# Sliding-window attention in 64-key half-blocks: 76 score batches instead of 96

## The chip, the core and the metric

The kernel runs on one core of a Trainium2 chip. The core has a matrix engine (TensorE, PE in the profile, with PEld for its weight loads), a vector engine (VectorE, DVE), a scalar engine (ScalarE, ACT), GpSimd (POOL) and SyncE (SP), which here only issues transfers. Each engine takes its own instructions in order and waits for the others by semaphores. TensorE reads SBUF and writes PSUM, which has eight banks of 128 partitions x 512 fp32 values. GpSimd works on SBUF alone. The metric is the device time of one execution in microseconds; less is better.

## The reference

One layer on 2048 rows of 512 values: layer norm, then attention and a gated unit side by side, added to the input.

```python
H = 32; Dh = 16; W = 256
xn = _layernorm(x)                                  # (1, 2048, 512)
qkv = (xn @ wqkv).reshape(B, S, 3, H, Dh).transpose(2, 0, 3, 1, 4)
scores = einsum("bhqd,bhkd->bhqk", q, k) * Dh ** -0.5
mask = (i - j >= 0) & (i - j < W)                   # query i, key j
p = softmax(where(mask, scores, -1e9))
attn = einsum("bhqk,bhkd->bhqd", p, v).transpose(0, 2, 1, 3).reshape(B, S, D) @ wo
g, u = xn @ w_gate, xn @ w_up                       # F = 1792
out = x + attn + (g * u) @ w_down
```

All inputs and the output are bf16. A query sees its own key and the 255 before it, so a block of 128 keys is seen by three blocks of 128 queries: a lower triangle, a full block and an upper triangle.

## The kernel before

**Chunks and banks.** The 2048 rows are taken in four chunks T of 512, that is four blocks of 128. Q, K, V and the transposed normed input of a chunk stay in SBUF. PSUM is split by hand: four banks hold one batch of scores (`ps_s`, one buffer), one bank the value sums (`ps_a`, the tile `accb`), and three banks (`ps_m`) everything else, in turn.

**Score batches (`scores`, line 214).** Heads are taken eight at a time, as a group c of 128 channels, four at once: e = 0..3 sits in channels 32e to 32e + 31, and `par` says whether the first or the second 16 of these are used (Ko is K with the first 16 zeroed). A step is (T, c, par, i). For each of the three entries i of `GROUPS` it takes two (key block, first and last query block, column) parts, which together make up to 512 columns for each e. Four matmuls of a part, one for each e, work in four row tiles of the array and write four different banks. One exp over all columns (line 231) makes the strip P in SBUF, and GpSimd zeroes the triangles in P with `affine_select`, 128 columns x 4 at a time (lines 236 and 240). There are 24 steps a chunk, 96 in all; in the first chunk the parts with keys before row 0 are missing.

**Value phases (`values`, line 245).** After the third step of a (T, c, par), and two steps later (`LAG = 2`), its three strips are multiplied by V: six parts of 128 to 384 columns, four matmuls each, one in each column tile, summed in `accb`. V has a column of ones, so the sums of the softmax come out beside the values. VectorE then transposes `accb` (at, line 263), takes the reciprocal (rz, line 265), and `divide` (line 268) multiplies (on, line 276) and, for each second phase, transposes back into OT (line 279). There are 32 value phases.

**Fillers.** All other matmuls form a fixed list: the Q, K and V projections of a chunk, the gate and up products, the down product and the output projection. A gate bank is four matmuls of 512 columns and is copied to SBUF as gsb by VectorE (line 294); an up bank is multiplied with gsb into hT by VectorE (line 304); K and Q banks are copied by VectorE (lines 182 and 188, and Ko at line 183); V banks by ScalarE (line 169). Down and output projection share one bank for 18 matmuls (lines 317 and 323) and end in y, on VectorE (line 341). `run` (line 424) walks the steps and after each one calls `fill`, which takes items off the list until the work given out, in units of one filler matmul, reaches a due point: the total times the share of the steps' weights done so far. A score step counts `SCORES` = 1.85 and a value phase `VALUES` = 3.5. Some items carry a step before which they must be done, or a value phase after which they may start. So the order of every engine is fixed when the program is built; nothing is reordered on the chip except weight loads.

Of the kernel before, what the change touches and what calls it, by code (L numbers as in the profile page):

```python
# [12 lines left out]

GROUPS = (
    ((-2, 0, 0, 0), (0, 0, 2, 128)),
    ((-1, 0, 1, 0), (2, 2, 3, 256)),
    ((1, 1, 3, 0), (3, 3, 3, 384)),
)  # L20


class Kernel:
    def __init__(self, ctx, tc, x, wqkv, wo, wg, wu, wd, out):
        self.tc, self.nc = tc, tc.nc
        _, S, D = x.shape
        self.S, self.D, self.F = S, D, wg.shape[1]
        assert D == 512 and S % 512 == 0 and self.F % 256 == 0
        self.NT, self.NCH, self.NF = S // 128, S // 512, self.F // 128
        self.x_d, self.out_d = x.flatten_outer_dims(), out.flatten_outer_dims()  # L30
        self.w_d = dict(qkv=wqkv, o=wo, g=wg, u=wu, d=wd)

        def pool(name, bufs, **kw):
            return ctx.enter_context(tc.tile_pool(name=name, bufs=bufs, **kw))

        self.const = pool("const", 1)
        self.chunk2 = pool("chunk2", 2)
        self.chunk3 = pool("chunk3", 3)
        self.ppool = pool("ppool", 6)
        self.work = pool("work", 3)  # L40
        self.xpool = pool("xpool", 4)
        self.small = pool("small", 4)
        self.ypool = pool("ypool", 5)
        self.ps_s = pool("ps_s", 1, space=bass.MemoryType.PSUM)
        self.ps_a = pool("ps_a", 1, space=bass.MemoryType.PSUM)
        self.ps_m = pool("ps_m", 3, space=bass.MemoryType.PSUM)


    def setup(self):
# [44 lines left out]
        nc.vector.tensor_copy(out=self.odd[:], in_=podd[:])  # L94
        self.mhalf = const.tile([128, 4], F32, name="mhalf")
        nc.gpsimd.memset(self.mhalf[:], -0.5)
        self.xnT, self.Q, self.hT, self.O, self.OT = {}, {}, {}, {}, {}
        self.K, self.Ko, self.V = {}, {}, {}
        self.strips, self.at = {}, {}

    def new_chunk(self, T):

        self.Q[T] = self.chunk2.tile([128, 4, 512], BF16, tag="Q", name=f"Q{T}")
        self.K[T] = self.chunk3.tile([128, 4, 512], BF16, tag="K", name=f"K{T}")
        self.Ko[T] = self.chunk3.tile([128, 4, 512], BF16, tag="Ko", name=f"Ko{T}")
        self.V[T] = self.chunk3.tile([128, 4, 32, 18], BF16, tag="V", name=f"V{T}")
        self.nc.gpsimd.memset(self.V[T][:, :, :, 16:18], 1.0)


    def norm_stats(self, t, n=4):  # L110
# [79 lines left out]
    def first_chunk(self):  # L190

        self.new_chunk(0)
        for b in range(2):
            self.norm_stats(b, 1)
            self.norm_scale(b, 1)
        for b in range(4):
            self.norm_apply(b)
            if b < 2:
                self.norm_stats(b + 2, 1)
                self.norm_scale(b + 2, 1)  # L200
        self.norm_transpose(0, False)
        for b in range(4):
            if b < 3:
                self.norm_transpose(b + 1, False)
            self.proj_v(b)
        self.proj_qk(0, 0, 1)
        self.proj_qk(0, 0, 0, on_act=True)
        self.proj_qk(0, 1, 1)


    def parts(self, T, i):
        return [p for p in GROUPS[i] if 4 * T + p[0] >= 0]

    def scores(self, T, c, par, i):

        nc = self.nc
        parts = self.parts(T, i)
        S = self.ps_s.tile([128, 4, 512], F32, tag="S", name="S")
        for kb, q0, q1, col in parts:
            n, (U, j) = 128 * (q1 - q0 + 1), divmod(4 * T + kb, 4)  # L220
            for e in range(4):
                rows = slice(32 * e, 32 * e + (32 if par else 16))
                nc.tensor.matmul(S[:, e, col:col + n],  # L223
                                 lhsT=(self.Ko if par else self.K)[U][rows, c, 128 * j:128 * j + 128],
                                 rhs=self.Q[T][rows, c, 128 * q0:128 * q0 + n],
                                 start=True, stop=True, tile_position=(32 * e, 0),
                                 skip_group_check=True)
        P = self.ppool.tile([128, 4, 512], BF16, tag="P", name="P")
        lo = parts[0][3]
        hi = parts[-1][3] + 128 * (parts[-1][2] - parts[-1][1] + 1)  # L230
        nc.scalar.activation(out=P[:, :, lo:hi], in_=S[:, :, lo:hi], func=ACT.Exp, scale=0.25)  # L231
        for kb, q0, q1, col in parts:
            for q in range(q0, q1 + 1):
                j = col + 128 * (q - q0)
                if q == kb:
                    nc.gpsimd.affine_select(out=P[:, :, j:j + 128], in_=P[:, :, j:j + 128],  # L236
                                            pattern=[[0, 4], [1, 128]], compare_op=ALU.is_ge,
                                            fill=0.0, base=0, channel_multiplier=-1)
                elif q == kb + 2:
                    nc.gpsimd.affine_select(out=P[:, :, j:j + 128], in_=P[:, :, j:j + 128],  # L240
                                            pattern=[[0, 4], [-1, 128]], compare_op=ALU.is_gt,
                                            fill=0.0, base=0, channel_multiplier=1)
        self.strips[(T, c, par, i)] = P

    def values(self, T, c, par):


        nc = self.nc
        acc = self.accb
        first = True  # L250
        for i in range(3):
            P = self.strips.pop((T, c, par, i))
            for kb, q0, q1, col in self.parts(T, i):
                n, (U, v) = 128 * (q1 - q0 + 1), divmod(4 * T + kb, 4)
                for e in range(4):
                    nc.tensor.matmul(acc[32 * e:32 * e + 17, 128 * q0:128 * q0 + n],  # L256
                                     lhsT=self.V[U][:, v, 8 * c + 2 * e + par, 0:17],
                                     rhs=P[:, e, col:col + n], start=first, stop=(i == 2),
                                     tile_position=(0, 32 * e), skip_group_check=True)
                first = False  # L260

        at = self.work.tile([128, 16, 32], F32, tag="at", name="at")
        nc.vector.transpose(out=at.rearrange("p b r -> p (b r)"), in_=acc[:])  # L263
        rz = self.small.tile([128, 16], F32, tag="rz")
        nc.vector.reciprocal(out=rz[:], in_=at[:, :, 16])
        self.at[(T, c, par)] = at, rz
# [78 lines left out]
    def fillers(self):  # L345


        out = []
        NCH, NF, NG = self.NCH, self.NF, 24

        def add(cost, f, before=None, after=None):
            out.append((cost, f, before, after))
# [8 lines left out]
        def project(T):  # L361
            add(0, lambda: self.new_chunk(T))
            for b in range(4):
                for ks in halves:
                    add(2, lambda t=4 * T + b, ks=ks: self.proj_v(t, ks), NG * T)
            for c in range(4):
                qk(T, c, NG * T + 6 * c)

        def gu(T, between):
            for f in range(NF):  # L370
# [20 lines left out]
                add(2, lambda lo=lo: self.down(T, b, lo, lo + 2))  # L391

        def wo(T, b, cs):
            add(len(cs), lambda: self.wo(T, b, cs), None, NG * T + 6 * cs[-1] + 5)

        qk(0, 1, 6, (0,))
        for c in range(2, 4):
            qk(0, c, 6 * c)
        for T in range(NCH):
            todo = {}  # L400
            if T:
# [22 lines left out]
    def run(self):  # L424
        self.xns, self.stats, self.sums = {}, {}, {}
        self.setup()
        NCH, NG, LAG = self.NCH, 24, 2
        RESERVE = 38
        self.first_chunk()
        steps = [(T, c, par, i) for T in range(NCH) for c in range(4) for par in range(2) for i in range(3)]  # L430
        weight = [sum(p[2] - p[1] + 1 for p in self.parts(s[0], s[3])) + 1.7 for s in steps]
        SCORES, VALUES = 1.85, 3.5
        work = self.fillers()
        total = sum(w[0] for w in work) - RESERVE + SCORES * len(steps) + VALUES * (len(steps) // 3 - 1)
        done_w, spent, n = 0, 0, 0
        valued = -1

        def fill(upto, group):
# [11 lines left out]

        def values(g):
            nonlocal spent
            if g < 0 or steps[g][3] < 2:
                return False
            self.values(*steps[g][:3])
            spent += VALUES
            return True

        def divide(g):
            nonlocal valued  # L460
            self.divide(*steps[g][:3])
            valued = g

        for g, s in enumerate(steps):
            fill(-1, g)
            self.scores(*s)
            spent += SCORES
            done_w += weight[g]
            upto = total * done_w / sum(weight)
            if values(g - LAG):  # L470
                fill(min(spent + 4, upto), g)
                divide(g - LAG)
            fill(upto, g)
        T = NCH - 1
        fill(spent + 20, -1)
# [48 lines left out]
```

The softmax here doesn't subtract the row's maximum and nothing guards it: scores larger than these inputs give would overflow.

## Time and profile before

| | |
|---|---|
| median of 3 runs | 279.97 us (279.86 to 280.08) |
| span of the profiled execution | 277.8 us |
| time around the span, against the median | 2.2 us |
| score batches, value phases | 96, 32 |
| score and value matmuls | 704, 704 |
| TensorE instructions in the program | 4,830 |
| granted TensorE clock | full in all stages |

The profile is of one execution. Busy times of TensorE are modelled from the size of a matmul, and a matmul's own duration (0.38 us for 512 columns) is longer than the distance to the next one, since they overlap. Starts are what was recorded, so the cost of a run of matmuls is read here from the distances between starts. A group's row gives line, engine, operation, tiles and shape, the count, then busy time and the mean of one in ns, then the idle time of its engine ahead of it and what ended most of that.

The stages by time, from the lines that ran: Q, K and V of the first chunk to 19 us, then for each chunk gate and up (19 to 51, 88 to 119, 155 to 186 and 223 to 255 us), the next chunk's projections (to 67, 134 and 202 us) and the down products (to 88, 154 and 221 us); the last down products run to 273 us.

### The profile page before, as it was taken

The numbers are of one execution on the slowest core, as the hardware profiler recorded it, in microseconds if no ns is written. First come the engines' busy times: TensorE is split into PE (matmuls) and PEld (weight loads), VectorE is DVE, ScalarE is ACT, GpSimd is POOL, SyncE is SP. The second block draws the span as 40 slices with busy tenths as digits, with TensorE's granted clock in tenths as the row PEclk, the third lists the DMA queues.
The fourth block names the chain that finished last, engine by engine and source line by source line (L and its number), as shares of the span: only waits on it lengthen the run. The fifth ranks groups of instructions, "written<-read, shape, count | busy, mean of one in ns | idle before, by whom it ended". The sixth has DMA issues, their size and how long they took to land.

```text
span 277.8 us, 5829 instructions
## 1 busy us (share of the span) xinstructions
PE 269.4 (97%) x2396; PEld 115.0 (41%) x2414; DVE 188.1 (68%) x338; ACT 183.1 (66%) x121; POOL 164.3 (59%) x284
## 2 busy tenths in 40 slices
PE   7999999999999999999999999999999999999994
PEld 6433433433344434343444344444434444433453
DVE  6388989788567777858855778774853477777232
ACT  3666766786767666688666676769676766767601
POOL 4146666765786656574777656575656566656510
PEclk9999999999999999999999999999999999999999
DMA  6999511000111100000012200000001000000002
GB/s 211 377 371 348 113 21 21 19 2 0 39 40 57 21 2 0 1 2 0 2 40 61 53 2 2 0 2 1 0 2 40 19 21 1 2 0 2 0 2 76
DMA packets 17163, 13.74 MB, mean 49 GB/s; under 512 B 7025, under 2 KB 17137, under 8 KB 17137
## 3 DMA queue, kind: packets, MB, share of 16 engines
q1 hardware_dynamic: 16848, 13.18, 15.6%
q8 instruction: 19, 0.31, 0.5%
q10 hardware_dynamic: 288, 0.20, 0.2%
q14 instruction: 8, 0.06, 0.1%
HBM read 9.70 MB, written 2.10 MB: 42 GB/s over the span
## 4 chain that ended last, share of the span: by engine, by line
PE 89%; ACT 5%; DVE 3%; issue 1%; DMA 1%; POOL 0%; ACTq 0%
PE up L300 18%; PE gp L289 18%; PE psd L317 18%; PE S L223 11%; PE qkp L177 9%; PE accb L256 8%; PE psd L323 5%; ACT P L231 3%; PE vp L165 3%; ACT V L169 1%; DMA x<-in_A_x_dram 1%; DVE st L116 1%; DVE hT L304 0%; DVE gsb L294 0%; PE xTp L151 0%
## 5 line engine op out<-in xcount | busy, mean ns | idle before, releaser
L231 ACT ACTIVATE P<-S 128x2048 bf16<-128x2048 f32 (+2 forms) x96 | 170.0, 1771 | 74.3 <-PE S L223 62.6
L236 POOL TENSOR_SCALAR_AFFINE_SELECT P<-P 128x512 bf16<-128x512 bf16 x128 | 84.7, 662 | 54.3 <-ACT P L231 54.1
L240 POOL TENSOR_SCALAR_AFFINE_SELECT P<-P 128x512 bf16<-128x512 bf16 x112 | 72.5, 647 | 38.4 <-ACT P L231 38.4
L300 PE MATMUL up<-xnT,Wu 128*128 128x512 bf16 x224 | 60.0, 380 | 0.1
L289 PE MATMUL gp<-xnT,Wg 128*128 128x512 bf16 x224 | 59.7, 380 | 0.0
L317 PE MATMUL psd<-Wd,hT 128*128 128x512 bf16 (+1 forms) x225 | 52.3, 366 | 1.4 <-issue 1.1
L263 DVE STREAM_TRANSPOSE at<-accb 128x512 f32<-128x512 f32 x32 | 22.8, 713 | 39.0 <-PE accb L256 39.0
L304 DVE TENSOR_TENSOR hT<-up,gsb 128x512 bf16<-128x512 f32 x56 | 38.1, 680 | 7.8 <-PE up L300 5.8
L294 DVE CAST gsb<-gp 128x512 bf16<-128x512 f32 x56 | 37.9, 676 | 5.9 <-PE gp L289 5.8
L317 PEld LDWEIGHTS <-hT 128*128 128x128 bf16 x238 | 21.5, 98 | 24.9 <-issue 4.7
L289 PEld LDWEIGHTS <-Wg 128*128 128x128 bf16 x224 | 20.0, 98 | 26.1 <-issue 5.2
L177 PE MATMUL qkp<-xnT,Wqkv 128*128 128x512 bf16 x128 | 30.6, 380 | 0.0
L300 PEld LDWEIGHTS <-Wu 128*128 128x128 bf16 x224 | 19.6, 98 | 26.4 <-issue 7.0
L256 PE MATMUL accb<-P,V 128*17 128x384 bf16 (+2 forms) x704 | 25.3, 276 | 0.0
L341 DVE TENSOR_TENSOR y<-psd,x 128x512 bf16<-128x512 f32 (+1 forms) x15 | 9.9, 666 | 17.9 <-PE psd L323 16.5
L223 PE MATMUL S<-Q,K 16*128 16x256 bf16 (+2 forms) x352 | 18.4, 276 | 0.5
L223 PE MATMUL S<-Q,Ko 32*128 32x256 bf16 (+2 forms) x352 | 18.4, 275 | 0.5 <-ACT P L231 0.2
L276 DVE TENSOR_TENSOR on<-at,rz 128x256 bf16<-128x256 f32 x32 | 18.1, 565 | 0.4
L177 PEld LDWEIGHTS <-Wqkv 128*128 128x128 bf16 x128 | 11.4, 98 | 14.6 <-issue 2.7
L256 PEld LDWEIGHTS <-V 128*17 128x17 bf16 x704 | 13.8, 90 | 8.7 <-issue 5.3
L182 DVE CAST K<-qkp 128x512 bf16<-128x512 f32 x16 | 11.0, 688 | 8.9 <-PE qkp L177 8.6
L323 PE MATMUL psd<-Wo,OT 128*128 128x512 bf16 (+1 forms) x67 | 16.6, 367 | 0.2 <-issue 0.2
(39 smaller groups left out, 141.1 us busy)
## 6 DMA issues: line engine op xcount, KB each, us to landing
Wg<-in_B_w_gate_dram SPq DMA_DIRECT2D x2, 896.0 KB, 10.1
Wu<-in_B_w_up_dram SPq DMA_DIRECT2D x2, 896.0 KB, 11.6
Wd<-in_B_w_down_dram SPq DMA_DIRECT2D x1, 1792.0 KB, 15.9
out_dram<-y SPq DMA_DIRECT2D x14, 128.0 KB, 1.7
Wqkv<-in_A_wqkv_dram SPq DMA_DIRECT2D x3, 512.0 KB, 5.5
x<-in_A_x_dram SPq DMA_DIRECT2D x1, 1024.0 KB, 10.5
x<-in_A_x_dram SPq DMA_DIRECT2D x1, 512.0 KB, 10.9
Wo<-in_A_wo_dram SPq DMA_DIRECT2D x1, 512.0 KB, 15.9
```

The source lines that it names most:

```text
L177: nc.tensor.matmul(ps[:], lhsT=self.Wqkv[:, k, lo:lo + 128], rhs=self.xnT[T][:, :, k, :], start=(k == 0), stop=(k == 3))
L223: nc.tensor.matmul(S[:, e, col:col + n], lhsT=(self.Ko if par else self.K)[U][rows, c, 128 * j:128 * j + 128], rhs=self.Q[T][rows, c, 128 ...
L231: nc.scalar.activation(out=P[:, :, lo:hi], in_=S[:, :, lo:hi], func=ACT.Exp, scale=0.25)
L236: nc.gpsimd.affine_select(out=P[:, :, j:j + 128], in_=P[:, :, j:j + 128], pattern=[[0, 4], [1, 128]], compare_op=ALU.is_ge, fill=0.0, base ...
L240: nc.gpsimd.affine_select(out=P[:, :, j:j + 128], in_=P[:, :, j:j + 128], pattern=[[0, 4], [-1, 128]], compare_op=ALU.is_gt, fill=0.0, bas ...
L256: nc.tensor.matmul(acc[32 * e:32 * e + 17, 128 * q0:128 * q0 + n], lhsT=self.V[U][:, v, 8 * c + 2 * e + par, 0:17], rhs=P[:, e, col:col + ...
L289: nc.tensor.matmul(ps[:], lhsT=self.Wg[:, k, 128 * f:128 * f + 128], rhs=self.xnT[T][:, :, k, :], start=(k == 0), stop=(k == 3))
L294: nc.vector.tensor_copy(out=self.gsb[:], in_=ps[:])
L300: nc.tensor.matmul(ps[:], lhsT=self.Wu[:, k, 128 * f:128 * f + 128], rhs=self.xnT[T][:, :, k, :], start=(k == 0), stop=(k == 3))
L304: nc.vector.tensor_tensor(out=self.hT[T][:, f, :], in0=ps[:], in1=self.gsb[:], op=ALU.mult)
L317: nc.tensor.matmul(ps, lhsT=self.hT[T][:, f, 128 * b:128 * b + 128], rhs=self.Wd[:, f, c0:c1], start=(f == 0), stop=False)
L323: self.nc.tensor.matmul(ps, lhsT=self.OT[T][:, c, 128 * b:128 * b + 128], rhs=self.Wo[:, c, c0:c1], start=False, stop=(c == 3))
```

## The change

Scores are taken over half-blocks of 64 keys. Half h of a key block uses the 64 array columns from 64h on, so a matmul works in a tile of 32 rows x 64 columns, eight of which exist (four e, two halves). A half-block is seen by 320 queries in place of 384 for a whole block: a triangle of 64, 256 full, a triangle of 64. Both halves are placed so that the same column of the strip is the same query in the full part.

There are now three kinds of batches, each 4 x 512 columns. EVEN and ODD belong to one `par` and hold key blocks J - 2, J and J + 2 for J = 0 or 1 (the rest of older blocks included); PLAIN holds, for both `par` at once, two full 128 x 128 blocks. A chunk has EVEN, ODD (par 0), PLAIN, EVEN, ODD (par 1) for each c, the first chunk only the four others: 4 x 4 + 3 x 4 x 5 = 76 steps.

The masks change. VectorE takes the minimum of two 64-column triangles with a constant table `diag` of zeros and 2^126 in one instruction; GpSimd's `affine_select` does the others, 64 columns x 4 each, four in a batch (three in the first chunk). PLAIN batches are not masked.

Where a strip column belongs to different queries in the two halves, the value product needs only one of them. For this there are zero-padded copies of V: Vu holds the first 64 keys of each block and zeros for the rest, Vl0 and Vl1 (even and odd chunks) the last 64. `zero_halves` fills the zeros once on GpSimd, and `copy_halves` copies the half of each chunk's V on VectorE. A value phase has 16 pieces of 64 to 256 columns in place of six (12 in the first chunk, in place of four).

The planner counts every step alike: the due point after step g is the total times (g + 1) / 76. The pools work and ypool each have one buffer less.

```diff
-GROUPS = (
-    ((-2, 0, 0, 0), (0, 0, 2, 128)),
-    ((-1, 0, 1, 0), (2, 2, 3, 256)),
-    ((1, 1, 3, 0), (3, 3, 3, 384)),
-)
+EVEN, ODD, PLAIN = 0, 1, 2
+BIG = 2.0 ** 126
...
-        self.work = pool("work", 3)
+        self.work = pool("work", 2)
...
-        self.ypool = pool("ypool", 5)
+        self.ypool = pool("ypool", 4)
...
+    def zero_halves(self, j):
+
+        for h in (0, 1) if j == 0 else (1,):
+            self.nc.gpsimd.memset(self.Vh[j][h][64 - 64 * h:128 - 64 * h], 0.0)
+
+    def copy_halves(self, T):
+
+        for h in range(2):
+            rows = slice(64 * h, 64 * h + 64)
+            self.nc.vector.tensor_copy(out=self.Vh[T % 2][h][rows], in_=self.V[T][rows])
...
+    def batches(self, T):
+
+        if T == 0:
+            return [(EVEN, 0), (ODD, 0), (EVEN, 1), (ODD, 1)]
+        return [(EVEN, 0), (ODD, 0), (PLAIN, None), (EVEN, 1), (ODD, 1)]
+
+    def score_pieces(self, T, kind, par):
+
+        if kind == PLAIN:
+            return [(p, kb, h, q, 128, 256 * p + col)
+                    for p in range(2) for kb, q, col in ((-1, 0, 0), (2, 384, 128)) for h in (None,)]
+        J, q = kind, 128 * kind
+        if T == 0:
+            first = [(par, 2, 0, 384 + 64 * J, 64, 0), (par, 2, 1, 384 + 64 * J, 64, 0)]
+            second = [(par, J, 1, q + 64, 64, 64)]
+        else:
+            first = [(par, J - 2, 0, q, 64, 0), (par, J - 2, 1, q, 128, 0)]
+            second = []
+        return first + second + [
+            (par, J, 0, q, 320, 64), (par, J, 1, q + 64, 320, 128),
+            (par, J + 2, 0, q + 256, 128, 384), (par, J + 2, 1, q + 320, 64, 448)]
...
+        for p, kb, h, q, n, col in self.score_pieces(T, kind, par):
+            U, j = divmod(4 * T + kb, 4)
+            keys, outs = slice(128 * j, 128 * j + 128), slice(0, 128)
+            if h is not None:
+                keys, outs = slice(128 * j + 64 * h, 128 * j + 64 * h + 64), slice(64 * h, 64 * h + 64)
             for e in range(4):
-                rows = slice(32 * e, 32 * e + (32 if par else 16))
-                nc.tensor.matmul(S[:, e, col:col + n],
-                                 lhsT=(self.Ko if par else self.K)[U][rows, c, 128 * j:128 * j + 128],
-                                 rhs=self.Q[T][rows, c, 128 * q0:128 * q0 + n],
-                                 start=True, stop=True, tile_position=(32 * e, 0),
+                rows = slice(32 * e, 32 * e + (32 if p else 16))
+                nc.tensor.matmul(S[outs, e, col:col + n],
+                                 lhsT=(self.Ko if p else self.K)[U][rows, c, keys],
+                                 rhs=self.Q[T][rows, c, q:q + n],
+                                 start=True, stop=True, tile_position=(32 * e, outs.start),
                                  skip_group_check=True)
...
+        both = P.rearrange("p e (b x) -> p e b x", x=64)[:, :, 1:7:5, :]
+        m = self.diag[:, 0:2, :] if T == 0 else self.diag[:, 1:3, :]
+        nc.vector.tensor_tensor(out=both, in0=both, in1=m.unsqueeze(1).to_broadcast([128, 4, 2, 64]),
+                                op=ALU.min)
+        for col in (320,) if T == 0 else (0, 320):
+            nc.gpsimd.affine_select(out=P[:, :, col:col + 64], in_=P[:, :, col:col + 64],
...
+        for col in (128, 448):
+            nc.gpsimd.affine_select(out=P[:, :, col:col + 64], in_=P[:, :, col:col + 64],
...
+    def value_pieces(self, T, kind, par):
+
+        if kind == PLAIN:
+            return [(256 * par, 2, -1, 0, 128), (256 * par + 128, 2, 2, 384, 128)]
+        J, q = kind, 128 * kind
+        if T == 0:
+            first = [(0, 2, 2, 384 + 64 * J, 64)]
+        else:
+            first = [(0, 2, J - 2, q, 64), (64, 1, J - 2, q + 64, 64)]
+        return first + [(64, 0, J, q, 64), (128, 2, J, q + 64, 256), (384, 1, J, q + 320, 64),
+                        (384, 0, J + 2, q + 256, 64), (448, 2, J + 2, q + 320, 64)]
...
+            V = self.V[U] if h == 2 else self.Vh[U % 2][h]
+            for e in range(4):
+                nc.tensor.matmul(acc[32 * e:32 * e + 17, q:q + n],
+                                 lhsT=V[:, v, 8 * c + 2 * e + par, 0:17],
+                                 rhs=P[:, e, col:col + n], start=(i == 0), stop=(i == len(todo) - 1),
+                                 tile_position=(0, 32 * e), skip_group_check=True)
...
-            done_w += weight[g]
-            upto = total * done_w / sum(weight)
+            upto = total * (g + 1) / len(steps)
             if values(g - LAG):
                 fill(min(spent + 4, upto), g)
                 divide(g - LAG)
+                T, c, par = due[g - LAG]
+                if (c, par) == (3, 1):
+                    self.copy_halves(T + 1)
             fill(upto, g)
```

## The prediction

> **What bounds the kernel now.** I read the busy times first, then the chain that ended last, then the costliest groups, one stretch of TensorE in order of time, and the stages.
>
> ```profile
> PE 269.4 (97%) x2396; PEld 115.0 (41%) x2414; DVE 188.1 (68%) x338; ACT 183.1 (66%) x121; POOL 164.3 (59%) x284
> PE 89%; ACT 5%; DVE 3%; issue 1%; DMA 1%; POOL 0%; ACTq 0%
> ```
>
> TensorE is busy almost all the time and is 89% of the chain; no transfer is on it. So only what shortens or interrupts TensorE moves the end, and time taken from ScalarE (66%) or GpSimd (59%) alone is worth nothing.
>
> ```profile
> L231 ACT ACTIVATE P<-S 128x2048 bf16<-128x2048 f32 (+2 forms) x96 | 170.0, 1771 | 74.3 <-PE S L223 62.6
> L236 POOL TENSOR_SCALAR_AFFINE_SELECT P<-P 128x512 bf16<-128x512 bf16 x128 | 84.7, 662 | 54.3 <-ACT P L231 54.1
> L300 PE MATMUL up<-xnT,Wu 128*128 128x512 bf16 x224 | 60.0, 380 | 0.1
> L304 DVE TENSOR_TENSOR hT<-up,gsb 128x512 bf16<-128x512 f32 x56 | 38.1, 680 | 7.8 <-PE up L300 5.8
> L294 DVE CAST gsb<-gp 128x512 bf16<-128x512 f32 x56 | 37.9, 676 | 5.9 <-PE gp L289 5.8
> ```
>
> The last column matters: TensorE waits 0.1 us before all 224 up matmuls, so VectorE always empties the banks in time today. VectorE never waits for an exp; only GpSimd (the masks) does.
>
> ```profile
> 100.83 0.59 PE L289 MATMUL gp<-xnT,Wg 128*128 128x512 bf16 x2
> 101.36 0.40 PE L223 MATMUL S<-Q,K 16*128 16x256 bf16 x8
> 101.68 0.83 PE L256 MATMUL accb<-P,V 128*17 128x128 bf16 x24
> 102.45 0.61 PE L289 MATMUL gp<-xnT,Wg 128*128 128x512 bf16 x2
> ```
>
> A score batch takes 0.32 us from its first start to the next phase's, a value phase 0.77. Over all 96 batches and 32 value phases the starts add to 30.5 and 24.8 us. Filler matmuls of 512 columns start 0.216 us apart. Four matmuls on the four row or column tiles start within some 10 ns and stream together, so 512 columns of a batch are 0.213 us of streaming; the other 0.11 is the change of array shape, and the filler run after it pays about 0.11 more.
>
> ```profile
> 19.00:51.00 32.00, 31.85 (x267) 12.44 (x266) 28.89 (x54) 20.62 (x16) 21.52 (x38) 1.00 0.45 130
> 88.00:119.00 31.00, 30.96 (x295) 12.73 (x292) 23.53 (x39) 21.33 (x12) 18.70 (x31) 1.00 0.04 10
> ```
>
> These are the first two gate/up stages (length, then busy PE, PEld, DVE, ACT, POOL). VectorE is at 90% in the first and 76% in the second, against 68% over the span.
>
> **The change, part by part.** The sum starts at 280.0, the median of the runs; the profiled span is 277.8, so 2.2 lie around it, and I leave those alone.
>
> *Batches, 76 for 96.* Twenty batches fewer save two shape changes each, 20 x 0.22 = 4.5 us. Streamed columns per row tile fall from 72 x 512 + 8 x (384 + 256 + 512) = 46,080 to 76 x 512 = 38,912 if the two halves stream at once: 7,168 / 2.4 per ns = 3.0 us. Together -7.5. If the halves stream one after the other, 64 batches take 0.213 longer: +13.6. The trace has no tile of 64 columns; the nearest rows, four row tiles or four column tiles, overlap fully, so I take overlap and keep the other end.
>
> *More and shorter matmuls.* Score matmuls go from 704 to 1,792 (24 or 28 in a half-block batch, 16 in a plain one), value matmuls from 704 to 1,920 (16 pieces a phase, 12 in the first chunk, for 6 and 4), each with a weight load. Their columns stay 1,536 per full value phase, so what is added is per piece. A set of four 128-column value matmuls takes 61 ns for 53 of streaming, longer ones 3 ns over. There are 24 x 10 + 8 x 8 = 304 more sets: 0.8 us at 2.5 ns; 10.3 us if a 64-column set (27 ns) can be no shorter than the 61 of the shortest seen. I take 5 ns, 1.5 us, as streaming set every interval seen, and 1 us for starting 24 score matmuls in place of 8.
>
> The Trainium skill's page "TensorEngine Tiling (Array Packing)", section Instruction Overhead, speaks against this part: about 60 cycles for each matmul whatever its size, so small free sizes gain nothing. By it, as an estimate, 3,712 small matmuls cost 93 us, some 40 over what I count. The rows above pay it once a set, not once a matmul, and I go by them.
>
> TensorE alone: 280.0 - 7.5 + 2.5 = 275.0.
>
> *ScalarE and GpSimd.* Exps: 76 x 1.88 = 143 us for 170. Masks: 240 selects of 256 elements for 240 of 512; at 0.29 us for 128 elements and 0.65 for 512, about 0.41, so 98 us for 157. Both are off the chain and worth nothing. The zero fills and the mask table add some 5 us on GpSimd at the start (0.33 us for 256 elements, two fills of 2,304 there), before the first values need them; at most 1 us shows.
>
> *VectorE: a new instruction that waits.* Each of 64 half-block batches gets a `min` of 512 bf16 elements with a table. Rows: 0.44 us (Ko, one tensor in) to 0.68 (hT, two, one from PSUM); I take 0.55, the other 512-element SBUF row (xn). 64 x 0.55 = 35 us. The copies into zero-padded V are 8 of 2,304 elements: 1.5 us each at Ko's slope, 3.0 at a PSUM cast's; 12 us, at chunk borders, where down matmuls need little of VectorE. VectorE goes from 188 to 235 us. The Trainium skill's page "VectorE: DVE Perf Modes" (perf-mode tier table) lets bf16 tensor_tensor in SBUF run at 2x; by it I estimate 0.42 for the `min`, 8 us less in all.
>
> The `min` stands in VectorE's queue right after its batch, so it waits for that batch's exp: in the trace exp starts about 0.53 after the first score matmul and takes 1.88, so the `min` cannot start for 2.4 us. Behind it are queued at, rz, and the gsb, hT, K and Q copies of everything that TensorE makes meanwhile. TensorE has three banks for that, 0.86 us each, and then stands. That is the cover, and I count whether it holds stage by stage, in the built order:
>
> - First gate/up stage: 10 `min`, 27 copies at 0.68, 5 value tails (at 0.71, rz 0.25, on 0.57), 2 OT, four norms: 38.5 us of VectorE. TensorE: 112 x 0.216 + 10 x 0.43 + 5 x 0.87 = 32.9. Over by 5.6.
> - The other three: 28.0, 29.5, 30.9 against TensorE's 30.7, 31.6, 32.0: 91 to 97% with in-order waits. A cycle worked by hand: scores end at 0, `min` 2.1 to 2.65, three copies to 4.7; TensorE has filled three banks by 2.6, does the next batch and wants the first bank at 3.0, free at 3.4: 0.4 lost. With a value tail ahead of the copies it is about 1.5, partly won back a batch later. Some 2 us per five batches, 10 batches a stage: 4 each, of which I take 3.5 for catching up, 10.5 in all.
> - Q/K projections: eight banks are 6.9 us of TensorE and 4 x (0.69 + 0.44 + 0.68) = 7.2 of VectorE before any `min`: 1 us in each of three chunks, 3 in all.
>
> Sum +19, with ends 3 (a `min` of 0.44, banks absorb nearly all) and 31 (0.68, no catching up). 275 + 19 = **294 us**.
>
> *Bookkeeping.* Due points are per step now, SCORES and VALUES unchanged; two work buffers for three and four y buffers for five cost nothing while gsb is used up within two banks. No DMA is added, and SP's queue keeps its order.
>
> **The rivals.**
> - *Faster: the banks absorb it.* If `min` costs 0.44 and VectorE's backlog hides the wait for exp, TensorE's sum stands: 275. For it: 0.1 us waited before 224 up matmuls today, and ScalarE freer. Against: 38.5 in 32.9 us cannot be absorbed.
> - *Slower by TensorE's instruction supply.* TensorE's instructions go from 4,830 to 9,438, and a batch with its value phase from 64 to 176. The densest stretch seen is those 64 in 1.09 us, 17 ns each, at streaming's pace. It decides from 1.09 / 176 = 6.2 ns an instruction on. At 12 ns: 2.1 for 1.09 us in 32 clusters (+33) and 0.58 for 0.33 in 44 lone batches (+11); with some VectorE stall left (6), 325. At 17 ns it would be 357. For it: no sustained rate beyond 58 ns is in the trace. Against: no wait of that kind shows in the dense stretches.
> - *Halves not at once.* +13.6, less 4 of VectorE's stall that then hides: 304.
>
> **How the numbers follow.** Forecast 0.47 (own range 283 to 306), absorbed 0.20, no change 0.03, supply 0.17, halves 0.13. The time is the forecast's, 294. The range 276 to 325 leaves out the better half of the absorbed case and the worse half of supply, some 0.2. Runs of this kernel differ by 0.1%, so 0.2% is what can be told from no change. Faster 0.20, same 0.03, slower 0.77.
>
> **What would show it.** Right: the gate/up and Q/K groups of TensorE get idle time released by gsb, hT, K or Q, several us in all; the `min` row shows idle before it released by ScalarE; VectorE passes 85%; TensorE's share of the span falls. A score batch of about 0.33 us and a value phase near 0.8 confirm streaming; 0.55 for the batch means halves in turn; 1.5 or more for the value phase means supply. Wrong: idle before gate and up matmuls stays near 0.1 us and the time is below 279.

## The result and the profile after

The changed kernel takes 317.5 us (median of four runs, 316.7 to 319.2); the kernel before took 280.0 beside it. The ratio is 1.135, with a 95% interval of 1.132 to 1.139: slower by 37.5 us. The profiled execution has a span of 317.1 us.

First the lines of its page that answer to those shown of before: busy times, the chain, then the groups.

```profile
PE 279.7 (88%) x4718; PEld 130.0 (41%) x4718; DVE 210.0 (66%) x410; ACT 156.6 (49%) x101; POOL 130.9 (41%) x291
...
PE 48%; DVE 26%; ACT 21%; issue 2%; POOL 2%; DMA 1%; ACTq 0%
...
L269 ACT ACTIVATE P<-S 128x2048 bf16<-128x2048 f32 x76 | 142.6, 1877 | 136.5 <-PE S L263 100.1
...
L278 DVE TENSOR_TENSOR P<-P,diag 128x512 bf16<-128x512 bf16 x64 | 27.9, 436 | 83.4 <-ACT P L269 83.4
L358 PE MATMUL up<-xnT,Wu 128*128 128x512 bf16 x224 | 59.7, 381 | 10.0 <-DVE gsb L352 9.7
L347 PE MATMUL gp<-xnT,Wg 128*128 128x512 bf16 x224 | 60.5, 384 | 6.7 <-DVE hT L362 6.6
...
L195 PE MATMUL qkp<-xnT,Wqkv 128*128 128x512 bf16 x128 | 32.7, 392 | 6.9 <-DVE Q L206 4.7
...
L381 PE MATMUL psd<-Wo,OT 128*128 128x512 bf16 (+1 forms) x68 | 17.6, 371 | 3.8 <-DVE OT L337 3.8
```

TensorE is no longer the bound: 88% busy and only 48% of the chain, where it was 89%. No other engine is full either. VectorE is at 66%, less than before's 68%. The row of L278 points to the reason: the new `min` is only 27.9 us of work, but VectorE stood idle 83.4 us ahead of it, all of it for exp. The last column of TensorE's rows shows who paid. The gate, up, Q and K matmuls now wait for the VectorE copies that free their banks (hT, gsb, Q), and the output projection waits for OT. The up matmuls waited 0.1 us before and 10.0 now.

One such wait in the changed kernel's timeline (start, length, engine, operation; the bracket is the idle time ahead and its releaser):

```profile
86.26 1.88 ACT L269 ACTIVATE P<-S 128x2048 bf16<-128x2048 f32 x1 [2.00 <-PE S L263]
...
87.11 0.81 PE L381 MATMUL psd<-Wo,OT 128*128 128x512 bf16 x3
88.17 0.43 DVE L278 TENSOR_TENSOR P<-P,diag 128x512 bf16<-128x512 bf16 x1 [2.03 <-ACT P L269]
...
88.51 0.71 DVE L321 STREAM_TRANSPOSE at<-accb 128x512 f32<-128x512 f32 x1
...
89.25 0.25 DVE L323 RECIPROCAL rz<-at 128x16 f32<-128x16 f32 x1
89.54 0.42 DVE L334 TENSOR_TENSOR on<-at,rz 128x256 bf16<-128x256 f32 x1
90.00 0.71 DVE L337 STREAM_TRANSPOSE OT<-on 128x512 bf16<-128x512 bf16 x1
...
90.77 0.61 PE L381 MATMUL psd<-Wo,OT 128*128 128x512 bf16 x1 [2.84 <-DVE OT L337]
```

The value phase had ended at about 86.7, so `at` could have begun then. But the `min` stood ahead of it until exp ended at 88.14. All four instructions of the tail came after it, and TensorE waited 2.84 us for OT.

Windows of the changed kernel (length, then busy time and count of PE, PEld, DVE, ACT, POOL; granted TensorE clock as a share of full speed, DMA share, GB/s); the first two are wide stretches, the last three were picked out by their clock:

```profile
16.00:56.00 40.00, 33.90 (x580) 14.98 (x583) 31.34 (x61) 18.43 (x10) 16.40 (x35) 0.96 0.43 132
72.00:92.00 20.00, 14.22 (x214) 5.87 (x212) 15.42 (x29) 7.01 (x4) 9.34 (x18) 0.87 0.01 2
...
21.80:25.20 3.40, 3.40 (x9) 1.05 (x7) 2.84 (x6) 0.00 (x0) 0.06 (x1) 0.51 1.10 347
76.40:79.90 3.50, 3.50 (x82) 1.56 (x79) 2.45 (x5) 0.74 (x1) 0.00 (x0) 0.51 0.02 5
90.10:96.90 6.80, 6.13 (x29) 2.13 (x30) 3.80 (x7) 1.88 (x1) 0.93 (x3) 0.50 0.15 39
```

In three stretches, 13.7 us together, the clock granted to TensorE was half. Each begins within 1.3 us of the end of a long wait of TensorE, so these waits were paid twice. With TensorE busy for most of those stretches, this is up to 6 or 7 us of this execution, the slowest of the four (319.2 us, mean clock 0.976). The fastest, 316.7 us, has 0.986: 3.2 us less of missing clock (the span times what the clock lacks of 1) go with 2.5 us less time. In the executions of run 6 below, 1.8 us of missing clock cost 1.6 to 1.8 us. The two middle executions lack 5.0 and 6.0 us of clock; by these two rates the clock is an estimated 4 to 5.5 us of the median's 37.5.

What the change did to the matmuls themselves is seen in one score batch and value phase of the changed kernel:

```profile
107.42 0.43 PE L263 MATMUL S<-Q,K 16*64 16x64 bf16 x24
107.77 0.32 PE L315 MATMUL accb<-P,V 128*17 128x128 bf16 x12
107.92 0.20 PE L315 MATMUL accb<-P,Vl 128*17 128x64 bf16 x4
107.95 0.20 PE L315 MATMUL accb<-P,Vu 128*17 128x64 bf16 x4
...
108.56 0.82 PE L381 MATMUL psd<-Wo,OT 128*128 128x512 bf16 x3
```

From start to next start, 24 score matmuls take 0.35 us and the 64 value matmuls 0.79. A set of four 64-column matmuls starts about 0.03 us after the one before.

### The profile page after: what moved, and what is told of

It is laid out like the page before. It is cut to its first block, busy times and chain, and to the rows that moved or that the text cites. A ratio compares the mean times of both kernels' runs of the same rounds, so it can differ in the third digit from the quotient of the medians.

```text
span 317.1 us, 10496 instructions
## 1 busy us (share of the span) xinstructions
PE 279.7 (88%) x4718; PEld 130.0 (41%) x4718; DVE 210.0 (66%) x410; ACT 156.6 (49%) x101; POOL 130.9 (41%) x291
## 4 chain that ended last, share of the span: by engine, by line
PE 48%; DVE 26%; ACT 21%; issue 2%; POOL 2%; DMA 1%; ACTq 0%
ACT P L269 21%; PE psd L375 16%; PE S L263 7%; PE up L358 6%; PE gp L347 6%; DVE at L321 4%; DVE P L278 4%; PE psd L381 4%; PE qkp L195 4%; DVE gsb L352 3%; PE accb L315 3%; DVE hT L362 3%; DVE OT L337 2%; PE vp L183 2%; DVE on L334 2%
## 5 line engine op out<-in xcount | busy, mean ns | idle before, releaser
L269 ACT ACTIVATE P<-S 128x2048 bf16<-128x2048 f32 x76 | 142.6, 1877 | 136.5 <-PE S L263 100.1
L281 POOL TENSOR_SCALAR_AFFINE_SELECT P<-P 128x256 bf16<-128x256 bf16 x112 | 57.3, 530 | 149.4 <-ACT P L269 149.4
L278 DVE TENSOR_TENSOR P<-P,diag 128x512 bf16<-128x512 bf16 x64 | 27.9, 436 | 83.4 <-ACT P L269 83.4
L375 PE MATMUL psd<-Wd,hT 128*128 128x512 bf16 (+1 forms) x238 | 56.3, 380 | 1.2 <-DVE hT L362 0.6
L285 POOL TENSOR_SCALAR_AFFINE_SELECT P<-P 128x256 bf16<-128x256 bf16 x128 | 54.5, 447 | 0.0
L352 DVE CAST gsb<-gp 128x512 bf16<-128x512 f32 x56 | 37.5, 670 | 0.7 <-PE gp L347 0.7
L358 PEld LDWEIGHTS <-Wu 128*128 128x128 bf16 x224 | 20.6, 98 | 37.5 <-issue 15.8
L315 PE MATMUL accb<-P,V 128*17 128x64 bf16 (+2 forms) x960 | 26.5, 222 | 0.0
L315 PE MATMUL accb<-P,Vu 128*17 128x64 bf16 x512 | 21.0, 194 | 0.0
L315 PEld LDWEIGHTS <-V 128*17 128x17 bf16 x960 | 17.3, 92 | 5.1 <-issue 0.7
L315 PE MATMUL accb<-P,Vl 128*17 128x64 bf16 x448 | 19.1, 194 | 0.0
L263 PE MATMUL S<-Q,Ko 32*64 32x64 bf16 (+3 forms) x896 | 17.5, 239 | 0.0
L263 PE MATMUL S<-Q,K 16*64 16x64 bf16 (+3 forms) x896 | 17.3, 237 | 0.0
## 6 DMA issues: line engine op xcount, KB each, us to landing
Wd<-in_B_w_down_dram SPq DMA_DIRECT2D x1, 1792.0 KB, 15.8
Wo<-in_A_wo_dram SPq DMA_DIRECT2D x1, 512.0 KB, 15.8
```

Of the source, the lines that this page charges most:

```text
L263: nc.tensor.matmul(S[outs, e, col:col + n], lhsT=(self.Ko if p else self.K)[U][rows, c, keys], rhs=self.Q[T][rows, c, q:q + n], start=True ...
L269: nc.scalar.activation(out=P[:], in_=S[:], func=ACT.Exp, scale=0.25)
L278: nc.vector.tensor_tensor(out=both, in0=both, in1=m.unsqueeze(1).to_broadcast([128, 4, 2, 64]), op=ALU.min)
L281: nc.gpsimd.affine_select(out=P[:, :, col:col + 64], in_=P[:, :, col:col + 64], pattern=[[0, 4], [-1, 64]], compare_op=ALU.is_gt, fill=0.0 ...
L285: nc.gpsimd.affine_select(out=P[:, :, col:col + 64], in_=P[:, :, col:col + 64], pattern=[[0, 4], [1, 64]], compare_op=ALU.is_ge, fill=0.0, ...
L315: nc.tensor.matmul(acc[32 * e:32 * e + 17, q:q + n], lhsT=V[:, v, 8 * c + 2 * e + par, 0:17], rhs=P[:, e, col:col + n], start=(i == 0), st ...
```

## The experiments

All times are medians, beside runs of the kernel before on the same chip (279.7 to 280.1). Losses are counted from the run without the `min`, 278.0.

**1. The `min` left out.**

```diff
-        nc.vector.tensor_tensor(out=both, in0=both, in1=m.unsqueeze(1).to_broadcast([128, 4, 2, 64]),
-                                op=ALU.min)
```

> The changed kernel without VectorE's min: the two triangles it masks are left unmasked, all else stays. Theory W (the min's place in VectorE's queue, waiting for exp, holds back the copies that empty TensorE's banks): TensorE's waits for gsb, hT, K, Q and OT go, 274 to 280 us. Rival D (too much VectorE work, 28 us of min and 6 of copies): also near 276, so this run does not part W from D. Rival H (half-blocks: shorter pieces, more instructions, planner's new due points): the min is not the cause, 305 to 317 us.

278.0 us (ratio 0.993, 0.9915 to 0.9945); the two triangles stay unmasked in this run. TensorE's wait ahead of the up matmuls is gone (for what, us in total, times, the longest):

```profile
PE up L354 <- DVE gsb L348: 0.4, 2, 0.3
```

One instruction in each of 64 batches carries the whole loss, 39.6 us, and nothing is left of a loss in the matmuls.

**2. The same `min`, issued later.** It stands just ahead of the next batch's scores, behind the copies and the value tail of its step.

```diff
         for g, s in enumerate(steps):
             fill(-1, g)
+            if g:
+                self.late_min(*steps[g - 1])
             self.scores(*s)
```

(shown without the lines that leave `scores`, those of run 1, and without the call for the last batch)

> The changed kernel with the same 64 min instructions, each issued just ahead of the next batch's scores instead of behind its own exp. Same work, same result, other place in VectorE's queue. Theory W: exp is done or nearly done when VectorE reaches the min, 276 to 285 us, and the min's idle time released by ScalarE falls from 83 us to under 25. Rival D: the work is the same, so 310 to 317 us. Rival H: 310 to 317 us.

279.7 us (0.9992, 0.9982 to 1.0002). Busy times and the row of the `min` in this run:

```profile
PE 266.9 (96%) x4718; PEld 128.3 (46%) x4718; DVE 213.7 (77%) x410; ACT 156.4 (56%) x101; POOL 125.1 (45%) x291
...
L291 DVE TENSOR_TENSOR P<-P,diag 128x512 bf16<-128x512 bf16 x64 | 29.1, 455 | 6.2 <-ACT P L269 6.1
```

The same 64 instructions, 29.1 us of them, now wait 6.2 us in place of 83.4, and 1.7 us of the loss is left. So the work, with what wait is left, costs 1.7 and the position 37.9. VectorE does slightly more in this run and is busier, and the kernel is 38 us faster: its load was never the trouble.

**3 and 4. The wait, and the work, put into the kernel before.** Two of its three batches in a group get a `min` that changes no value, once on the strip that exp writes and once on a tile that nothing else uses.

```diff
+        if i != 1:
+            both = P.rearrange("p e (b x) -> p e b x", x=64)[:, :, 2:8:5, :]
+            m = self.diag[:, 0:2, :]
+            nc.vector.tensor_tensor(out=both, in0=both, in1=m.unsqueeze(1).to_broadcast([128, 4, 2, 64]),
+                                    op=ALU.min)
```

(in run 4 `self.scr` for `P`)

> The kernel before with 64 added VectorE min instructions on 128 columns x 4 of the strip, right behind the exp of steps i = 0 and 2, against a table of 2^126, so that nothing changes in the values. Theory W: the stall appears without half-blocks, 300 to 320 us, with TensorE's idle time before gate and up matmuls above 10 us. Rival D: VectorE at 216 of 280 us, 300 to 320 too. Rival H: 280 to 283 us.

> The kernel before with the same 64 min instructions at the same places of VectorE's queue, but on a scratch tile that nobody else touches, so that none waits for exp. Theory W: 280 to 286 us. Rival D: as the run before, 300 to 320 us. Rival H: 280 to 283 us.

296.9 us (1.061, 1.0593 to 1.0625) with the wait, 283.3 (1.012, 1.0103 to 1.0133) without. The rows of the run with the wait:

```profile
L237 DVE TENSOR_TENSOR P<-P,diag 128x512 bf16<-128x512 bf16 x64 | 27.9, 436 | 52.1 <-ACT P L233 51.9
L307 PE MATMUL up<-xnT,Wu 128*128 128x512 bf16 x224 | 60.0, 380 | 5.0 <-DVE gsb L301 4.1
L296 PE MATMUL gp<-xnT,Wg 128*128 128x512 bf16 x224 | 59.6, 380 | 5.2 <-DVE hT L311 2.6
```

The mechanism works without the half-blocks, but the wait costs 13.6 us here, under what was expected, and not 37.9. The number of filler matmuls behind a batch with a `min` hardly differs: 10.6 in the mean of chunks 1 to 3, for 11.0 in the changed kernel (12.8 behind an EVEN batch, 9.0 behind an ODD one). But in the kernel before the value tail falls in the step without a `min`, so it seldom stands right behind the wait, while in the changed kernel it falls at the ODD steps, which all have one. And VectorE idles only 52.1 us here, for 83.4. Runs 5, 6 and 9 to 12 look at the wait, the tail and the fillers.

**5. The wait made shorter.** Exp is cut in three, with the columns that the `min` needs first.

```diff
-        nc.scalar.activation(out=P[:], in_=S[:], func=ACT.Exp, scale=0.25)
...
+        Pb, Sb = (t.rearrange("p e (b x) -> p e b x", x=64) for t in (P, S))
+        for cut in (slice(1, 7, 5), slice(0, 8, 7), slice(2, 6)):
+            nc.scalar.activation(out=Pb[:, :, cut, :], in_=Sb[:, :, cut, :], func=ACT.Exp, scale=0.25)
```

(PLAIN batches keep the single exp)

> The changed kernel with the min at its place in VectorE's queue, but the exp of a half-block batch cut in three: first the 2 x 64 columns that the min needs (about 0.6 us), then 128, then 256 columns. Same VectorE work and order; the wait behind which the copies stand falls from about 2.4 us after the first score matmul to about 1.2. Theory W: the loss goes with the length of the wait, 283 to 297 us, VectorE's idle time released by ScalarE under 35 us. Rival D and rival H: 315 to 318 us.

282.9 us (1.0112, 1.0099 to 1.0126), at the good end of the expectation. VectorE still idles 43.3 us ahead of the `min`, more than expected, and still the loss falls from 39.6 to 4.9 us. Half the idle time costs an eighth. That fits a cover: what does harm is the part of a wait that is longer than what TensorE's banks bridge. No run changes the number of banks, so this reason is argued, not shown; run 6 adds to it.

**6. The `min` behind the value tail of its step, but still ahead of the remaining copies.**

```diff
             if values(g - LAG):
                 fill(min(spent + 4, upto), g)
                 divide(g - LAG)
+            self.late_min(*s)
             fill(upto, g)
```

(shown without the copies of V, which stay where they are, and without the lines that leave `scores`, those of run 1)

> The changed kernel with the min behind the value tail (at, rz, on, OT) of the same step, still ahead of the copies of most fillers made after the batch. Theory W has two ways for the loss: the copies of TensorE's banks are held back (then 300 to 312 us, most of the loss stays), or the value tail and with it OT and the output projection are (then 280 to 292 us). I take the first to be the larger.

299.3 us (1.068, 1.066 to 1.0707): between the two expectations. The row of the `min`:

```profile
L291 DVE TENSOR_TENSOR P<-P,diag 128x512 bf16<-128x512 bf16 x64 | 31.2, 487 | 43.4 <-ACT P L269 43.2
```

The move is worth 18.2 us and 21.3 are left, but it does more than put the tail first. In the trace 43.3 us of the idle time lie ahead of the 32 EVEN `min` and 0.1 ahead of the 32 ODD ones (38.1 and 45.3 in the changed kernel): by the time the tail and the copies of the next four fillers are done, exp is too. So the wait itself is gone from the ODD steps, off the tail and off the copies alike, and this run does not part the two. The 21.3 are the EVEN waits, about as in run 11 below.

Beside run 5 it says more. VectorE idles the same 43 us ahead of the `min` in both, in run 5 in 64 waits of 0.68 us in the mean, in run 6 in 32 of 1.35, and the loss is 4.9 and 21.3 us: the length of the single wait counts, not the sum. Part of the 18.2 is the clock: the mean granted clock is 0.994 in the profiled execution here and 0.976 in that of the changed kernel, which is 1.8 and 7.6 us of missing clock, so at most 5.8.

**7. The late `min`, and the zero fills in four pieces.** In the run without the `min` one start-up line stood out: the fourth norm's xn. Its neighbourhood there, and then in this run:

```profile
8.36 2.18 DVE L153 TENSOR_SCALAR xn<-x,mv,rs 128x512 bf16<-128x512 bf16 x1 [0.76 <-POOL rs L145]
8.38 2.01 POOL L119 MEMSET Vu<- 64x2304 bf16 x1
...
10.60 0.40 PE L169 MATMUL xTp<-ident,xn 128*128 128x128 bf16 x4 [1.28 <-DVE xn L153]
```

```diff
-            self.nc.gpsimd.memset(self.Vh[j][h][64 - 64 * h:128 - 64 * h], 0.0)
+            for b in range(4):
+                self.nc.gpsimd.memset(self.Vh[j][h][64 - 64 * h:128 - 64 * h, b], 0.0)
```

> The kernel with the late min, and the two zero fills of 2,304 elements at the start, each one GpSimd instruction of 2.0 us, cut into four of 576. In the run without the min, a VectorE instruction of the fourth norm took 2.18 us, where it takes 0.41 elsewhere, while such a fill ran. If GpSimd's instruction held VectorE off, that one falls under 1.0 us and the kernel comes to 277.5 to 278.8 us, faster than both kernels. If it was chance or the fill as such, 279.3 to 280 us.

```profile
8.32 0.74 DVE L154 TENSOR_SCALAR xn<-x,mv,rs 128x512 bf16<-128x512 bf16 x1 [0.76 <-POOL rs L146]
8.35 2.27 POOL L120 MEMSET Vu<- 64x576 bf16 x4
...
9.13 0.40 PE L170 MATMUL xTp<-ident,xn 128*128 128x128 bf16 x4 [0.25 <-DVE xn L154]
```

278.6 us (0.9957, 0.9945 to 0.997). xn takes 0.74 us in place of 2.18, and 1.05 us is gained on run 2. This version is faster than both kernels, by 0.4% than the one before.

**8. The two triangles masked by GpSimd** (a product with a 0/1 table), so that VectorE has no new instruction but the copies.

```diff
-BIG = 2.0 ** 126
+BIG = 1.0
...
-        nc.vector.tensor_tensor(out=both, in0=both, in1=m.unsqueeze(1).to_broadcast([128, 4, 2, 64]),
-                                op=ALU.min)
+        nc.gpsimd.tensor_tensor(out=both, in0=both, in1=m.unsqueeze(1).to_broadcast([128, 4, 2, 64]),
+                                op=ALU.mult)
```

(the zero fills are in pieces here too)

> The split zero fills, and the two triangles masked on GpSimd by one multiplication with a table of zeros and ones instead of VectorE's min. VectorE then has no wait for exp and 28 us less work. Theory W: 275.5 to 278 us. If GpSimd, with 64 more instructions, holds VectorE off or is late for the values: 280 to 290 us.

283.6 us (1.0138, 1.0122 to 1.0153): the expectation was missed. The GpSimd row of this run's groups, and a VectorE row that shares the time with it:

```profile
L279 POOL TENSOR_TENSOR P<-P,diag 128x512 bf16<-128x512 bf16 x64 | 74.5, 1164 | 69.0 <-ACT P L270 68.8
...
L335 DVE TENSOR_TENSOR on<-at,rz 128x256 bf16<-128x256 f32 x32 | 27.1, 847 | 0.3
```

`on` takes 847 ns in the mean and Ko 741; in run 7 they took 472 and 437. GpSimd is not full (69%), but while it works, VectorE's instructions on SBUF take longer: with 29.2 us of `min` fewer, VectorE is busy 207.9 us for 212.3. The kernel loses 5.0 us on run 7. TensorE's waits in this run name no mask; it waits 2.8 us for gsb, where run 7 has 1.0. So late masks are not the reason.

**9 and 10. Fewer fillers behind a `min`, more behind PLAIN batches, with and without the `min`.**

```diff
+        weight = [1 if s[0] == 0 else 2.0 if s[2] == PLAIN else 0.75 for s in steps]
...
-            upto = total * (g + 1) / len(steps)
+            done_w += weight[g]
+            upto = total * done_w / sum(weight)
```

> The changed kernel with the min where the change put it, but with the fillers of chunks 1 to 3 given out unevenly: a due-point weight of 0.75 for an EVEN or ODD step and 2.0 for a PLAIN one, so that some 9 fillers stand behind a batch with a min in place of 12.8, and 27 behind a PLAIN batch in place of 12.7. Nothing is added or left out. Theory (three PSUM banks, 12 fillers, are the cover; what stands behind the min beyond them is stood still for): with 9 fillers the next batch and its value phase come before the banks run out, the loss against the same order without the min falls from 39.6 us to the 14 to 20 that the kernel before showed with 9.9 fillers a batch, and the time is 292 to 300. Rival (each min costs its 0.6 us whatever is behind it): the loss stays at 35 to 42 and the time at 313 or more.

> The same uneven order with the min left out (the two triangles that it masks stay unmasked). It is the base of the run before: both theories expect 277.5 to 281, since the order alone should cost TensorE nothing with VectorE and ScalarE far from full; if it is above 283, the uneven order has a price of its own, and only the difference between the two runs counts.

308.7 us (1.103, 1.1011 to 1.1048) and 281.3 (1.0052, 1.0037 to 1.0067). The loss in this order is 27.5 us for 39.6: neither theory's number. Fillers behind the wait are a part of the cost, about 12 us for three to four matmuls fewer a batch in chunks 1 to 3 (9.0 for 12.8 behind an EVEN batch, 5.7 for 9.0 behind an ODD one), but far from all.

**11 and 12. The `min` in the EVEN batches alone, or in the ODD ones alone.**

```diff
+        if kind == EVEN:
...
-        nc.vector.tensor_tensor(out=both, in0=both, in1=m.unsqueeze(1).to_broadcast([128, 4, 2, 64]),
+            nc.vector.tensor_tensor(out=both, in0=both, in1=m.unsqueeze(1).to_broadcast([128, 4, 2, 64]),
```

(run 12 has ODD in the first line)

> The changed kernel with the min in its place for the 32 EVEN batches alone (in the ODD batches the two triangles stay unmasked). In the built order the value phases, and with them the tail at, rz, on and OT, always come at an ODD step, so behind an EVEN min stand copies of filler banks alone. Theory (copies and tail each cost, about half and half): 32 waits without a tail cost 32/64 of the bank part of about 20 us, 10, less what is caught up in the ODD steps between: 283 to 289, and clearly less than the run with ODD alone. Rival (the tail is worth nothing, each wait costs the same): half of 39.6, 296 to 299, and the same in both runs.

> The same with the min in the 32 ODD batches alone (the two triangles of the EVEN batches stay unmasked): behind 31 of the 32 stands the tail of a value phase. Theory: the tail's part of 13 to 18 us and half of the bank part, 10, less what is caught up in the EVEN steps: 291 to 302, at least 6 above the run with EVEN alone. Rival: 296 to 299, as in the other run. If both runs lie below 285, a wait is caught up in the next step and it is their succession that costs; then the two losses add up to far less than 39.6.

295.9 us (1.056, 1.0522 to 1.0599) and 304.8 (1.0894, 1.0867 to 1.0921). The waits of TensorE in both runs (for what, us in total, times, the longest), EVEN first:

```profile
PE up L359 <- DVE gsb L353: 5.5, 7, 1.0
PE gp L348 <- DVE hT L363: 4.3, 6, 0.9
...
PE psd L382 <- DVE OT L338: 1.1, 1, 1.1
```

```profile
PE up L359 <- DVE gsb L353: 6.8, 10, 1.4
PE psd L382 <- DVE OT L338: 3.8, 2, 2.8
PE gp L348 <- DVE hT L363: 3.4, 6, 0.7
```

Thirty-two waits with only copies behind them cost 17.9 us, 0.56 each; thirty-two, all but one with the value tail behind them, 26.8, 0.84 each. The granted clock is 0.994 in both. So the ODD waits cost 9 us more, and the wait for OT rises from 1.1 to 3.8. The tail is the plain difference, but not the only one: VectorE idles 65.5 us ahead of the ODD `min` and 53.9 ahead of the EVEN ones, and fewer fillers stand behind an ODD batch. That all of the 9 us is the tail's is not shown. The EVEN run is far above the 283 to 289 expected: the bank part alone was under-estimated again. The two losses add up to 44.7, against 39.6 for both at once. If a batch without a `min` were used to catch up, each run alone would lose far less than its part; it is the other way round.

## Why the prediction went right in direction and wrong in size

Direction and mechanism were right, and 317.5 lies inside the range. The time of 294 was wrong: +37.5 us where +14 was forecast. By the prediction's own steps:

- *Batches and matmul pieces, 275.0 for TensorE alone.* Run 1 gives 278.0. The starts of score batches and value phases add to 51.0 us for 55.3 in the kernel before, so 4.2 of the 5.0 us came. The first exp starts at 15.8 us for 13.9, so the start-up gave 1.8 us back where "at most 1 us shows" was granted; the zero fills are 1.05 of it by run 7.
- *Rivals "instruction supply" and "halves not at once".* Both are refuted by the trace and by run 1: 0.35 us a batch and 0.79 a value phase, where they needed 0.55 or 0.58, and 1.5. Streaming sets the pace of the 64-column value matmuls too: a set of four every 29 ns, where 0.216 us for 512 columns makes 27.
- *Rival "banks absorb".* Refuted for the place where the `min` stands (run 1 against the changed kernel), true for the late place (run 2).
- *Prices of VectorE's new instructions.* They were too high: `min` 0.436 us for 0.55, the copies into V 0.77 and 0.79 for 1.5. VectorE does 210 us, not 235, and is at 66%, so the sign "passes 85%" was wrong. The estimate from the Trainium skill's page "VectorE: DVE Perf Modes" (perf-mode tier table), 0.42 us, was the nearer one for the `min`.
- *VectorE waits in order, +19 with ends 3 and 31.* This is the step that failed, by its size. Run 1 puts the whole term at 39.6 us, above the upper end; by run 2 the wait is 37.9 of it and the work 1.7. The prediction saw the right place and the right victims (gsb, hT, K, Q). Its parts, against what the profiled execution of the changed kernel has over that of run 1, from the first matmul of a stage to that of the next (us):

  | part | forecast | measured |
  |---|---|---|
  | first gate and up stage | 5.6 | 7.9 |
  | the other three | 10.5 | 15.4 |
  | projections of three chunks | 3 | 9.6 |
  | down products | 0 | 5.7 |
  | start-up | 0 | 2.3 |

  (The sum, 40.9, is that of the slowest of four executions.) The projections cost three times their price (one stretch of half clock is in them), and the down stages, at which nothing was put, 5.7; 4.6 of these fall in the first, with the 2.84 us wait for OT and the longest stretch of half clock. In the gate and up stages the loss of 0.4 us a batch, 1.5 with a value tail ahead of the copies, was cut by about half as "partly won back a batch later", and again from 4 to 3.5 a stage for catching up. Runs 11 and 12 show 0.56 and 0.84 us a wait and no catching up to speak of. Taken whole over the 64 waits, its own prices make some 60 us (33 at 0.4, 31 at 1.5), so the price with a tail was too high and what was taken off was far too much. The changed kernel pays 0.62 each; the forecast of 19 is 0.30 each.
- *What the tail and the clock add.* OT was not among the things that TensorE would wait for; 3.8 us of it show in the changed kernel, and 1.1 in run 1. The fall of the clock was not foreseen at all. By runs 11 and 12, copies alone would cost 36 us over 64 waits (twice 17.9) and the tails 9 more, 5 above what both cost at once; the clock's 4 to 5.5 us are inside these figures. If the copies behind an ODD wait cost what those behind an EVEN one do, the held copies are by far the largest part.
- *The check against the load was the wrong one.* The over-full first gate stage (38.5 in 32.9) was the strongest argument against "banks absorb". The late `min` loads VectorE alike and costs 1.7 us, so that argument decided nothing; by runs 5 and 6 the length of the single wait did.

What stays open: the exact share of the half clock, since no execution of the changed kernel has it at full (single ones of runs 6, 9 and 11 do, at 297.6, 307.3 and 294.8 us), and how the cost of one wait depends on the number of fillers behind it. Runs 3, 9 (counted from run 10) and 11 give 0.21, 0.43 and 0.56 us a wait for about 10.6, 7.4 and 12.8 fillers in chunks 1 to 3, but they also differ in the tail, in the length of a wait and in how the waits follow each other.

## What to carry to other kernels

An instruction that must wait for a long one on another engine costs little by its own length and much by what stands behind it in its engine's queue: count how long it waits, what is queued behind it (a chain that ends at the bounding engine, as at, rz, on and OT do, too) and how long the buffers last. Then put it behind everything that need not wait, here at the end of its step. A low share of busy time on that engine is no comfort. What one wait costs, and what is won back later, should both come from a run: here the prices worked by hand were wrong in both directions, and the discount for catching up was the larger error.

## What the runs showed of the hardware

- An instruction of GpSimd can hold an instruction of VectorE for its whole length. xn took 2.18 us under a memset of 2.01 (run 1) and 0.74 with the memset in pieces (run 7); on took 847 ns with GpSimd at 69% and 472 with it at 45% (runs 8 and 7). The Trainium skill's page "SBUF — State Buffer", section "SBUF: two separate sides", describes a port pair that the two engines share as an exclusive lock held for a whole instruction; these rows agree with it in the length. Which instruction came first the first pair does not tell, since their starts are 0.02 us apart.
- TensorE's granted clock fell to 0.50 or 0.51 within 1.3 us of the end of waits of 1.91, 2.49 and 2.84 us, for 3.4 to 6.8 us. Not every such wait brought it: in run 12 the clock stayed full at a wait of 2.8 us for OT, and the five executions of run 9's kernel have mean clocks from 0.988 to 1.0. The Trainium skill's page "TensorE: Matmul & The Clock Gate" (HAM oscillation) warns of idle gaps above about 3.4 us; here shorter ones preceded it, and the measurement decides.
- Value matmuls of 64 columns on four column tiles start a set of four every 29 ns or so, about the 27 ns of their streaming. On 32-row by 64-column tiles the two halves of a batch stream side by side: 24 score matmuls with twice 512 columns for each e take 0.35 us to the next start, where eight with once 512 took 0.32 in the kernel before.
